# Reordering the work around the weight fold of a linear attention with a linearised MoE

## The chip, the cores and the metric

One core of a Trainium2 chip. Times are device microseconds (us) of one execution. Engines: PE is TensorE (PEld its weight loads), DVE is VectorE, ACT is ScalarE, POOL is GpSimd, SP is SyncE. The clock is the share of TensorE's full clock that the profile shows as granted. An execution counts as slow when it is over 1.5% above the fastest of the same kernel. A ratio is the mean time of one kernel's fast runs over that of the other's in the same rounds, with a 95% interval, so it is not quite the ratio of the medians.

## The reference, cut to what matters

```python
# attention: 8 batches x 8 heads x 576 positions x 64
q_p, k_p = phi(q, cos, sin), phi(k, cos, sin)      # relu(x)*cos and relu(x)*sin, side by side
kv  = einsum('bhsf,bhsd->bhfd', k_p, v);  z = sum(k_p, axis=2)
x   = einsum('bhsf,bhfd->bhsd', q_p, kv) / (q_p . z + 1e-06)
# then a feed-forward layer over 4608 tokens of 512, d_ff 2048
out = softplus(x @ w_in) @ w_out
```

The kernel replaces softplus by its line through zero: `out = x @ W_c + bias` with `W_c = 0.5 * w_in @ w_out` (the fold, 64 matmuls) and a bias of ln 2 times the column sums of `w_out`. It squares x and the weights, and branches on their norms at the end to an exact path if the line isn't good enough.

## The kernel before: the parts in question

Batch 0 is worked while the weights arrive; then W_c is copied out of PSUM; then batch 1 starts; then 32 more tiles of 128 tokens follow. Each tile has a turn of the queries (PE, copied by ACT), an attend (PE), a reciprocal and a division (DVE), a turn of x (PE, ACT) and an emit (PE with W_c; DVE adds the bias). In these traces an engine's queue is worked in the order of the program: ACT's first copy of W_c starts at 42.01 us, behind six squares, though the fold ended at 40.93.

```python
def square_w(ft):                     # norms of the weights
    if ft % 2 or ft >= 10: nc.scalar.activation(..., ACT.Square, accum_out=...)
    else:                  nc.vector.scalar_tensor_tensor(...)

def pool_relu(b):                     # GpSimd rectifies keys and queries of batch b
    nc.gpsimd.tensor_copy(gate, vcs_bufs[(b - 1) % 2][:, 3, T - 1, 1, VW - 2 :])
    ...

for j in range(BLOCKS + 1):           # the fold, 8 blocks of weights
    if j < BLOCKS: turn_w_in(j)
    ...
    if 0 < j < 5: attend(j - 1, qt_ps)
    ...
    if j > 0:
        fold(j - 1, wc_ps)
        for ft in range(FB * (j - 1), FB * j): square_w(ft)
    if j in (3, 5): sum_w_out((j - 3) // 2)
    ...
for hq in range(2):                   # the passage into batch 1
    for c in range(2): scale_values(1, hq, c)     # DVE, "value products" vcs
relu_k(1, nc.vector)
for g in range(KO): ...               # W_c out of PSUM, ACT and DVE in turn
bias()
relu_q(1, 0, nc.gpsimd); relu_q(1, 1, nc.vector)
for hq in range(2): key_values(1, hq)             # PE
finish(*emit(0, xt_bank())); turn_queries(4, split=True)
finish(*emit(1));            turn_queries(5, big_ps)
pool_relu(2)
...
def pass_stores(i, rden):             # stores wait while loads last
    keep = HOLD - 1 - 3 * max(0, i - 27)
    if len(held) > keep: nc.sync.dma_start(passed[...], rden...)   # gate copy
    while len(held) > max(0, keep): store(*held.pop(0))
```

## Time and profile before

| | before |
|---|---|
| median of the first three runs | 138.13 us (137.68 to 140.26) |
| last fold matmul ends | 40.93 us |
| first key-value product of batch 1 | 43.45 us |
| reciprocal of tile 4, 8, 13, 35 | 47.96, 57.86, 71.89, 123.81 us |
| end of the span | 136.1 us |

Here is the passage in the timeline of the kernel before (start, length, engine, line, operation, output and inputs, count, and in brackets the idle time before it and what ended it):

```profile
38.59 2.76 DVE L286 TENSOR_TENSOR vcs<-v_sb,cs_wide 128x1152 bf16<-128x1152 bf16 x4 [0.65 <-DMA v_sb<-in_v_dram]
41.42 0.76 DVE L262 TENSOR_SCALAR k_sb<-k_sb 128x2304 bf16<-128x2304 bf16 x1
42.62 1.29 DVE L496 TENSOR_SCALAR W_c<-wc_ps 128x512 bf16<-128x512 f32 x2 [0.44 <-ACT W_c L498]
42.86 1.14 POOL L269 TENSOR_SCALAR q_r<-q_sb 128x1152 bf16<-128x1152 bf16 x1 [0.19 <-DMA q_sb<-in_q_dram]
43.45 1.25 PE L300 MATMUL kv_ps<-vcs,k_sb 64*64 64x132 bf16 x72
```

### The profile page before, as it was taken

How to read it: one execution, taken by the hardware profiler on the slowest of the kernel's cores; microseconds unless marked ns; L12 is line 12 of the kernel's file. 1: busy time of each engine (PE TensorE's matmuls, PEld its weight loads, DVE VectorE, ACT ScalarE, POOL GpSimd, SP SyncE). 2: the span in 40 equal slices, each digit the busy share in tenths (PEclk: the TensorE clock that was granted, in tenths of full speed). 3: DMA queues.
4: the chain of work that ended last, by engine and by line, in shares of the span. 5: the costliest groups of instructions: out<-in, count | busy, mean ns of one | idle time of the engine just before them, and what ended most of it. 6: DMA issues, size and time to landing. Idle time of an engine off the chain costs nothing.

```text
span 136.1 us, 4522 instructions
## 1 busy us (share of the span) xinstructions
PE 114.9 (84%) x1890; PEld 74.7 (55%) x1890; DVE 102.6 (75%) x219; ACT 94.5 (69%) x161; POOL 66.5 (49%) x83
## 2 busy tenths in 40 slices
PE   5926959999699998998969998999999999989400
PEld 2303636666345665764747775766767677655100
DVE  1499536797777689999978988898977996687600
ACT  3401493696698475989876996998997997987100
POOL 6994544645525029989889666159124800000000
PEclk9999999999999999999999999999999999999985
DMA  1999999999999999999999999999996365776480
GB/s 8 179 184 200 201 202 199 200 202 202 207 207 207 208 207 210 207 209 207 208 209 207 228 262 256 253 251 256 241 277 208 117 205 200 288 245 234 180 289 15
DMA packets 24779, 28.15 MB, mean 207 GB/s; under 512 B 1712, under 2 KB 20144, under 8 KB 24752
## 3 DMA queue, kind: packets, MB, share of 16 engines
q0 software_dynamic: 19136, 18.35, 82.3%
q1 hardware_dynamic: 5616, 9.44, 20.0%
q8 instruction: 17, 0.28, 0.8%
q14 instruction: 10, 0.08, 0.2%
HBM read 36.70 MB, written 9.44 MB: 339 GB/s over the span
## 4 chain that ended last, share of the span: by engine, by line
PE 49%; DVE 22%; ACT 15%; issue 6%; POOL 2%; ACTq 0%; POOLq 0%; DVEq 0%
PE o_ps L408 11%; PE q_ps L327 9%; DVE vcs L286 8%; ACT qT L339 8%; PE wc_ps L239 8%; PE kv_ps L300 6%; PE num_ps L357 5%; PE xT_ps L377 3%; DVE o_sb L426 3%; DVE x L368 3%; ACT xT_all L381 3%; ACT x L386 3%; DVE diag L161 2%; PE wT_ps L209 2%; PE o_big L408 1%
## 5 line engine op out<-in xcount | busy, mean ns | idle before, releaser
L339 ACT CAST qT<-q_ps 128x1024 bf16<-128x1024 f32 x34 | 34.3, 1014 | 8.2 <-PE q_ps L327 8.1
L408 PE MATMUL o_ps<-W_c,xT_all 128*128 128x512 bf16 x132 | 33.9, 379 | 0.8 <-DVE o_sb L426 0.7
L286 DVE TENSOR_TENSOR vcs<-v_sb,cs_wide 128x1152 bf16<-128x1152 bf16 x32 | 28.0, 891 | 0.6 <-DMA v_sb<-in_v_dram 0.6
L426 DVE TENSOR_TENSOR o_sb<-o_ps,b_bc 128x512 f32<-128x512 f32 x33 | 22.6, 686 | 7.4 <-PE o_ps L408 7.3
L368 DVE TENSOR_TENSOR x<-num_ps,rden 128x512 bf16<-128x512 f32 x36 | 24.9, 691 | 2.1
L262 POOL TENSOR_SCALAR k_sb<-k_sb 128x1152 bf16<-128x1152 bf16 x12 | 14.9, 1253 | 17.4 <-DMA k_sb<-in_k_dram 17.4
L327 PE MATMUL q_ps<-diag,q_r 128*128 128x256 bf16 x144 | 21.9, 274 | 1.6 <-issue 0.5
L381 ACT CAST xT_all<-xT_ps 128x512 bf16<-128x512 f32 x36 | 21.4, 596 | 1.2 <-PE xT_ps L377 1.2
L269 POOL TENSOR_SCALAR q_r<-q_sb 128x1152 bf16<-128x1152 bf16 x13 | 16.8, 1305 | 6.3 <-PE q_ps L327 3.4
L386 ACT ACTIVATE x<-x,zero_b 128x1024 bf16<-128x1024 bf16 x17 | 19.7, 1161 | 0.0
L408 PEld LDWEIGHTS <-xT_all 128*128 128x128 bf16 x144 | 12.7, 98 | 10.1 <-issue 1.1
L357 PE MATMUL num_ps<-kvblk,qT 64*128 64x65 bf16 (+1 forms) x640 | 15.7, 193 | 1.1 <-issue 1.1
L327 PEld LDWEIGHTS <-q_r 128*128 128x128 bf16 x144 | 11.7, 97 | 6.0 <-issue 2.0
L239 PE MATMUL wc_ps<-w_out_sb,w_inT 128*128 128x512 bf16 x64 | 15.0, 379 | 0.0
L300 PE MATMUL kv_ps<-vcs,k_sb 64*64 64x132 bf16 x576 | 11.4, 219 | 4.1 <-DVE vcs L286 4.1
L305 ACT CAST kvblk<-kv_ps 128x260 bf16<-128x260 f32 x16 | 6.0, 375 | 10.1 <-PE kv_ps L300 9.7
L377 PE MATMUL xT_ps<-perm,x 128*128 128x128 bf16 x128 | 12.4, 219 | 0.6 <-ACT xT_all L381 0.6
L300 PEld LDWEIGHTS <-k_sb 64*64 64x64 bf16 x576 | 9.1, 106 | 6.0 <-issue 4.3
L357 PEld LDWEIGHTS <-qT 64*128 64x128 bf16 (+1 forms) x640 | 11.3, 97 | 2.0 <-issue 1.1
L377 PEld LDWEIGHTS <-x 128*128 128x128 bf16 x144 | 10.6, 98 | 2.0 <-issue 0.6
L347 PEld LDWEIGHTS <-warm 128*128 128x128 bf16 x72 | 6.7, 98 | 8.8 <-issue 1.6
L436 PE MATMUL spin_ps<-warm 128*128 128x512 bf16 x28 | 8.6, 468 | 1.5 <-DVE warm L104 1.5
(76 smaller groups left out, 131.3 us busy)
## 6 DMA issues: line engine op xcount, KB each, us to landing
out_dram<-o_sb SPq DMA_DIRECT2D x32, 256.0 KB
v_sb<-in_v_dram POOLq DMA_DIRECT2D x7, 576.0 KB, 12.2
k_sb<-in_k_dram POOLq DMA_DIRECT2D x7, 576.0 KB, 14.8
q_sb<-in_q_dram POOLq DMA_DIRECT2D x6, 576.0 KB, 18.2
xT_all<-in_moe_w_in_dram POOLq DMA_DIRECT2D x8, 256.0 KB, 10.7
w_out_sb<-in_moe_w_out_dram POOLq DMA_DIRECT2D x8, 256.0 KB, 10.7
q_sb<-in_q_dram POOLq DMA_DIRECT2D x4, 288.0 KB, 10.3
out_dram<-o_sb SPq DMA_DIRECT2D x8, 128.0 KB
```

The costliest lines, as they stand in the source:

```text
L239: nc.tensor.matmul(ps[g // 2][:, g % 2, :], w_inT_rows(ft)[:, g * 128 : (g + 1) * 128], w_out_rows(ft)[:, 0], start=(ft == 0), stop=(ft == ...
L286: nc.vector.tensor_mul(view(vcs, [T * 2 * VW, 2], [2 * VW, T], [1, D], offset=2 * hq * T * 2 * VW + c * VW), kqv[b, "v"][:, 2 * hq : 2 * h ...
L300: nc.tensor.matmul(kv[64 * i : 64 * i + 64, h2, :, :VW], k_r[rows, 2 * hq + i, t, :], vcs[rows, 2 * hq + i, t, :, :], start=(t == 0), stop ...
L327: nc.tensor.matmul(ps[:, j // 2, 256 * (j % 2) : 256 * (j % 2) + 256], q_rs[b][:, hq, t, :, :], diag[:, t, :, :], start=True, stop=True, s ...
L339: nc.scalar.copy(view(qT, [512, 2], [64, 2], [128, 4], [1, 64]), view(ps, [1, 1024]))
L357: nc.tensor.matmul(num[p0 : p0 + m, i, C * g : C * g + C], qTs[n][rows, hq, 2 * c + h2, p0 : p0 + m], blk_bufs[b % 3][rows, hq, h2, c, :], ...
L368: nc.vector.tensor_mul(xs[n // 2][:, n % 2], view(num, [C, 4], [512, 2], [1, D]), view(rden, [1, 4], [4, 2], [0, D]),)
L377: nc.tensor.matmul(ps[:, g, :], x[:, g, :, :], perm if len(tiles[n]) == 1 else ident, start=True, stop=True, skip_group_check=True,)
L381: nc.scalar.copy(xT_all[:, n], ps)
L386: nc.scalar.activation(x, x, ACT.Square, bias=zero_b, accum_out=x_norm[:, n : n + 1])
L408: nc.tensor.matmul(ps, xT_all[:, n, g, :], W_c[:, g, :], start=(g == 0), stop=(g == 3))
L426: nc.vector.tensor_add(o_sb, ps, b_bc)
```

## The change

Its intent: start the fold sooner, get W_c out sooner by moving ACT's last squares behind it, use W_c at once for four emits, and drop the gate copies of the stores. Cut to the core, in five parts that the text names **head**, **squares**, **W_c first**, **four emits** and **stores** (a load in two parts, the last half store's move to ACT's queue and the numbering of the norm's steps are cut):

```diff
 # head
+            if t < 4:  (DVE)   else:  nc.scalar.mul(diag[:, t, c, :], ident, cs_col[...])
-        spin(5)
+        spin(5 - 2 * hq)
-    turn_queries(1, big_ps)
+    turn_queries(1, big_ps, split=True)
+        if j > 0:
+            fold(j - 1, wc_ps)
         if 0 < j < 5:
             attend(j - 1, qt_ps)
 # squares: 12, 13 behind the W_c copies, 14, 15 behind the turn of tile 5, x squares 0 and 1 later
-            if j % 2 == 1:
-                square_x((j - 3) // 2)
-            for ft in range(FB * (j - 1), FB * j):  square_w(ft)      # all j
+        if 0 < j < 6:  (the same)
+        if j == 7:     (weight squares 10, 11)
 # W_c first
-    for hq in range(2): ... scale_values(1, hq, c)
-    relu_k(1, nc.vector)
     for g in range(KO): ...  W_c
+    for ft in range(6 * FB, 7 * FB):
+        square_w(ft)
     bias()
+    square_x(0)
+    for hq in range(2): ... scale_values(1, hq, c)
+    relu_k(1, nc.vector)
     relu_q(1, 0, nc.gpsimd)
-    relu_q(1, 1, nc.vector)
 # four emits
+    early = [emit(0, xt_bank()), emit(1)]
     for hq in range(2):
         key_values(1, hq)
+    (finish both, relu_q(1, 1, nc.vector), emit 2, turn 4, emit 3, turn 5, finish both)
+    for ft in range(7 * FB, FO):
+        square_w(ft)
 # stores: one gate at tile 27, on the last query load; all held stores go then
+        if i == LAST_HELD:
+            nc.sync.dma_start(passed[...], kqv[B - 1, "q"][:1, 3, T - 1, :16])
+        while len(held) > (0 if i == LAST_HELD else HOLD - 1):
```

More of the change, by code (lines that the diff above doesn't have):

```diff
@@ L124 @@
     w_tmp = loads.tile([128, 2, D_MODEL], F32, tag="q", name="w_tmp", bufs=4)
-    load(1, "v")
+    for part in range(2):
+        load(1, "v", part)
     load(1, "k")
@@ L160, in mark_diag @@
         for c in range(2):
-            nc.vector.tensor_scalar_mul(diag[:, t, c, :], ident, cs_col[:, c, t : t + 1])
+            if t < 4:
+                nc.vector.tensor_scalar_mul(diag[:, t, c, :], ident, cs_col[:, c, t : t + 1])
+            else:
+                nc.scalar.mul(diag[:, t, c, :], ident, cs_col[:, c, t : t + 1])
     perm = singles.tile([128, 128], BF16)
@@ L401, in store @@
             else:
-                nc.sync.dma_start(rows[:, T - 1, :], o_sb[p0 : p0 + m])
+                (nc.scalar if p0 and n == last else nc.sync).dma_start(
+                    rows[:, T - 1, :], o_sb[p0 : p0 + m]
+                )
     def emit(n, ps=None):
@@ L413 @@
     HOLD = 11
+    LAST_HELD = last - 8
     held = []
@@ L417, in pass_stores @@
     def pass_stores(i, rden):
-        keep = HOLD - 1 - 3 * max(0, i - 27)
-        if len(held) > keep:
+        if len(held) < HOLD or i > LAST_HELD:
+            return
+        if i == LAST_HELD:
+            nc.sync.dma_start(passed[:, i % 4, :].bitcast(BF16), kqv[B - 1, "q"][:1, 3, T - 1, :16])
+        else:
             nc.sync.dma_start(passed[:, i % 4, :], rden[:1].rearrange("p i g -> p (i g)"))
-        while len(held) > max(0, keep):
+        while len(held) > (0 if i == LAST_HELD else HOLD - 1):
             store(*held.pop(0))
@@ L427, in finish @@
         held.append((n, o_sb))
-        if n > last - 3:
-            while held:
-                store(*held.pop(0))
+        while n >= LAST_HELD - 2 and held:
+            store(*held.pop(0))
     def spin(count, rhs=None):
@@ L444 @@
     mark_eps()
-    for t in range(4):
+    for t in range(T):
         mark_diag(t)
@@ L449 @@
             relu_k(0, nc.vector, slice(2, 4))
-            for t in range(4, 8):
-                mark_diag(t)
         for c in range(2):
             scale_values(0, hq, c)
-    for hq in range(2):
         key_values(0, hq)
-        spin(5)
+        spin(5 - 2 * hq)
     for hq in range(2):
@@ L459 @@
     mark_perm()
-    mark_diag(8)
     turn_queries(0, split=True)
-    turn_queries(1, big_ps)
-    wc_ps = [None]
+    turn_queries(1, big_ps, split=True)
+    xt_bank = lambda: xt_ps.tile([128, D_MODEL], F32, tag="xt", name="o_xt")
+    big_bank = lambda: big_ps.tile([128, 2, D_MODEL], F32, tag="big", name="o_big")[:, 0]
     for j in range(BLOCKS + 1):
@@ L470 @@
             nc.vector.tensor_copy(ident_f, ident)
-        if 0 < j < 5:
-            attend(j - 1, qt_ps)
         if j == 1:
@@ L476 @@
             ]
+        if j > 0:
+            fold(j - 1, wc_ps)
+        if 0 < j < 5:
+            attend(j - 1, qt_ps)
         if 1 < j < 6:
             turn_x(j - 2)
-            if j % 2 == 1:
-                square_x((j - 3) // 2)
-        if j > 0:
-            fold(j - 1, wc_ps)
+        if 0 < j < 6:
             for ft in range(FB * (j - 1), FB * j):
+                square_w(ft)
+        if j == 7:
+            for ft in range(FB * 5, FB * 6):
                 square_w(ft)
@@ L489 @@
             fetch(3)
-    for hq in range(2):
-        for c in range(2):
-            scale_values(1, hq, c)
-    relu_k(1, nc.vector)
     for g in range(KO):
@@ L498 @@
             nc.scalar.mul(W_c[:, g, :], wc_ps[g // 2][:, g % 2, :], 0.5)
+    for ft in range(6 * FB, 7 * FB):
+        square_w(ft)
     bias()
+    square_x(0)
+    for hq in range(2):
+        for c in range(2):
+            scale_values(1, hq, c)
+    relu_k(1, nc.vector)
     relu_q(1, 0, nc.gpsimd)
-    relu_q(1, 1, nc.vector)
+    early = [emit(0, xt_bank()), emit(1)]
     for hq in range(2):
         key_values(1, hq)
-    xt_bank = lambda: xt_ps.tile([128, D_MODEL], F32, tag="xt", name="o_xt")
-    finish(*emit(0, xt_bank()))
+    for done in early:
+        finish(*done)
+    relu_q(1, 1, nc.vector)
+    early = [emit(2, xt_bank())]
     turn_queries(4, split=True)
-    finish(*emit(1))
+    early.append(emit(3))
     turn_queries(5, big_ps)
+    for done in early:
+        finish(*done)
+    for ft in range(7 * FB, FO):
+        square_w(ft)
     pool_relu(2)
@@ L542 @@
                 turn_x(i - 1)
-            if i < last:
+            if 5 < i < last:
                 finish(*emit(i - 2))
+            if i == 4:
+                square_x(1)
             if i > 4 and i % 2 == 0:
                 square_x(i // 2 - 1)
-            if b == 1 and j < 2:
-                for _ in range(1 + j):
+            if b == 1 and 1 < j < 4:
+                for _ in range(j - 1):
                     next(w_steps)
         n = mine[-1] + 1
-    big_bank = lambda: big_ps.tile([128, 2, D_MODEL], F32, tag="big", name="o_big")[:, 0]
     emitted = [emit(last - 2)]
```

## The prediction

> **What bounds the kernel now.** I read the chain that ended last, then busy time by stretches of 5 us, then the timeline at the end of the weight fold, then the queue of the stores and the last branch. The kernel has three stages: batch 0 with the weight fold (0 to 43 us), a passage into batch 1 (43 to 50), and 32 tiles of steady work (to 127), followed by the end.
>
> ```profile
> PE 49%; DVE 22%; ACT 15%; issue 6%; POOL 2%; ACTq 0%; POOLq 0%; DVEq 0%
> ```
>
> No engine owns the chain. The stretches (columns: stretch, its length, busy us and instructions of PE, PEld, DVE, ACT, POOL, then clock, DMA share, GB/s) show why:
>
> ```profile
> 35.00:40.00 5.00, 3.93 (x25) 1.99 (x24) 3.39 (x11) 3.79 (x10) 1.88 (x3) 1.00 1.21 207
> 45.00:50.00 5.00, 5.00 (x65) 3.41 (x63) 3.54 (x8) 2.66 (x4) 0.00 (x0) 1.00 1.21 208
> 55.00:60.00 5.00, 5.00 (x143) 3.59 (x131) 4.93 (x9) 4.24 (x8) 4.42 (x7) 1.00 1.21 209
> 95.00:100.00 5.00, 4.88 (x87) 3.51 (x89) 4.86 (x10) 4.75 (x9) 0.65 (x1) 1.00 1.18 248
> 105.00:110.00 5.00, 4.83 (x108) 3.55 (x106) 4.86 (x9) 4.75 (x8) 2.76 (x2) 1.00 0.30 114
> ```
>
> In the steady part PE, DVE and ACT are all over 80% busy; slack lies only in the first 50 us. The DMA is saturated (share over 1) to 105 us: the loads keep about 203 GB/s from 3 us on, and the last load releases this:
>
> ```profile
> 105.62 2.76 POOL L269 TENSOR_SCALAR q_r<-q_sb 128x1152 bf16<-128x1152 bf16 x2 [2.06 <-DMA q_sb<-in_q_dram]
> ```
>
> Batch 7's queries are rectified at 108.38, and the first turn of them starts at 110.19 in the timeline. So the computing can come forward by about 1.8 us at most before it waits for the loads.
>
> At the fold, ScalarE is late: six weight squares run before the first copy of the folded weight, which starts at 42.01 although the fold ended at 40.93.
>
> ```profile
> 20.14 0.19 PE L347 MATMUL num_ps<-eps_b,warm 128*128 128x4 bf16 x2 [1.23 <-ACT qT L339]
> ...
> 36.87 0.61 PE L209 MATMUL wT_ps<-ident,xT_all 128*128 128x128 bf16 x8 [1.07 <-ACT w_inT L215]
> ...
> 41.29 0.72 ACT L224 ACTIVATE w_square<-w_inT,zero_b 128x512 bf16<-128x512 bf16 x1
> ...
> 42.01 1.06 ACT L498 ACTIVATE W_c<-wc_ps 128x512 bf16<-128x512 f32 x2
> ```
>
> At the end SP works through a backlog of gate copies and stores, while PE has a branch that takes 4.6 us:
>
> ```profile
> 126.74 0.69 SPq L420 DMA_DIRECT2D passed<-rden  x1
> 127.84 1.85 SPq L400 DMA_DIRECT2D out_dram<-o_sb  x3
> 129.79 1.21 SPq L402 DMA_DIRECT2D out_dram<-o_sb  x2
> ...
> L566 SPq TENSOR_LOAD <-fits x1: 732/732/732, 131.1 to 131.1; - x1
> ...
> L567 PEldq COMPARE_BRANCH  x1: 4586/4586/4586, 129.6 to 129.6; - x1
> ...
> L567 SPq EVENT_SEMAPHORE  x8: 17/17/17, 132.3 to 134.4; - x8
> ...
> L567 PEldq EVENT_SEMAPHORE  x1: 51/51/51, 134.3 to 134.3; - x1
> ```
>
> Two chains meet: SP's last wait (a store) passes at 134.4 and PE comes out of its branch at 134.3. Both must be done; 1.7 us later the span ends. I take this as the most important reading: shortening SP's chain alone wins almost nothing.
>
> [...] PE's 4.59 us, and 16 KB instruction packets at 131.6 to 132.8. [...] Here, under load, the last half store was issued at 130.40 and its wait passed near 134.3: 3.9 us. [...] The trace has 1.57 us for 8 diagonals on DVE (0.20 each); none on ACT yet. [...] the value multiplies take 0.69 alone, up to 1.62 beside GpSimd at 58.70.
>
> **The change part by part.**
>
> Head. Ten diagonals leave DVE: 8 x 0.17 + 2 x 0.20 = 1.8 us. They go to ACT, which idles until 11.00[...]. DVE had waited for nothing there, but query part two lands near 13.9, so its rectifying ends at about 14.6 against 14.68. With two spins fewer the first turn of queries starts near 14.7 against 15.37: -0.7. PE's wait of 1.23 us at 20.14 is filled with the first fold. From there the weight blocks land every 2.66 us and PE needs wT 0.45 + fold 1.73 + attend 0.36 + xT 0.33 = 2.87 us a block, so I get the copy of block 5 at 30.1 (was 31.7). Behind it the unchanged DVE run of a square and three sums, 4.1 us, still holds block 6. I get the last fold's end at 39.3 against 40.93: **-1.6**.
>
> Passage. ACT now has two squares ahead of W_c: W_c starts at 38.55, and DVE's last part ends at 40.45 (was 43.91). But DVE does the value multiplies (4 x 0.69) and the key rectifying (0.76) after W_c, not before, so these end at 43.95 (was 42.18). Then two emit additions (1.38) and the query part (0.75): 46.05. The turn of tile 4 comes at 46.1 (was 45.50), and attend of tile 4 at 48.05 (was 47.36): **+0.7**, but emits 2 and 3 are done, 2 x 0.86 = 1.7 us of PE and 2 x 0.69 = 1.4 us of DVE ahead. On work done PE stands 1.0 us ahead and DVE level.
>
> ACT pays. Four weight squares (0.85 each) and two x squares (1.25) come later. Two of the former and one of the latter stand behind the turn of tile 5: 1.7 + 1.25 = 2.95 us between copies for which PE waits, because there is one bank for the turned queries. Placing the copies (0.92 each in a row): tile 6 at 51.65, tile 7 at 53.8, tile 8 at 55.3. So emit 4 ends at 55.5 against 54.3, and its addition starts about 1.0 us later than 54.49. From there to tile 11 DVE sets the pace as before, then PE. **+1.0** on the end of the computing by this placing. I trust the placing to about 1 us, and its errors are one-sided: some value multiplies leave GpSimd's windows (about 0.3), and PE's lead on the emits lets some waits overlap (about 0.3). I take **+0.4**.
>
> Gates. SP loses 8 gate copies of 0.67 us after tile 27, and all held stores go after the last load. The idle DMA at 105 to 110 us is filled. 22 stores of 0.26 MB at the 290 GB/s that the trace shows in the fast slices take 20 us, from 106 to 126, so SP is free when the last tile is. SP's chain shortens by 131.05 - 128.75 = 2.3 us (its load of the flag against the other engines'). PE's branch remains. Its fetch might gain the wait of 2.0 us from branch to packet in part, and 0.2 us of its packet (1.18 against 0.95 elsewhere), as stores drain earlier. I take **-0.8** in all, of which 0.3 is safe.
>
> Sum: +0.4 - 0.8 = -0.4; 138.13 - 0.4 = **137.7 us**.
>
> **The rivals.**
>
> 1. The squares find holes and PE's lead counts in full: the computing is 1.5 us earlier. For it: ACT is only 2.66 of 5 us busy at 45 to 50. Against: it is in order, and the squares stand where PE waits. With the tail -0.8: 135.8 us. More is cut off by the loads (1.8 us).
> 2. The passage becomes the bound: ScalarE's squares hold the single bank, DVE idles, and the placing holds in full or grows [...]. +1.0 to +1.8, tail -0.3: 138.8 to 139.6 us.
> 3. The tail is all SP: if PE's branch is short once stores are gone, 2.3 us of gain: 136.2 us. For it: the fetch packets wait behind stores. Against: the same seconds of stores also run in the new kernel.
>
> **Range and chances.** The rivals span 135.8 to 139.6. Faster by over 2% means under 135.4, which needs rivals 1 and 3 together and the loads' limit just kept: 0.13. Slower by over 2%, over 140.9, needs rival 2 beyond its top: 0.06. Within 2%: 0.81. Eight in ten: 135.7 to 139.5.
>
> **What would show it.** The fold's last matmul near 39.3; W_c on ACT near 38.6; attend of tile 4 near 48; then ACT busy nearly without a gap from 48 to 57 and PE waiting for its query copies 2 to 3 us; SP's flag load with the other engines' at the end, and PE's branch still above 4 us and last. It would be wrong if tile 4 came before 47, if PE did not wait for ACT at 49 to 54, if PE's branch fell under 3 us, or if a wait for batch 7's queries showed up near 108.

## More of the kernel before

The reciprocal of a tile is a good milepost: each tile has one, on DVE, right behind its attend. How late a milepost is tells in which stage time was lost.

DVE does batch 1's value products while PE still folds, and is done before GpSimd rectifies queries at 42.86. The key-value products begin without a wait.

## The result, and the profile after

The changed kernel took **143.09 us** in the median (141.95 to 143.69, four runs); the kernel before took 138.45 beside it. Ratio 1.0345, interval 1.0249 to 1.044: **slower**. The profiled execution took 143.19 us, its span is 140.9.

| milepost, us | before | after | later by |
|---|---|---|---|
| last fold matmul ends | 40.93 | 40.77 | -0.2 |
| first key-value product of batch 1 | 43.45 | 46.47 | 3.0 |
| reciprocal of tile 4 | 47.96 | 51.58 | 3.6 |
| reciprocal of tile 8 | 57.86 | 62.95 | 5.1 |
| reciprocal of tile 35, the last | 123.81 | 130.15 | 6.3 |
| span's end | 136.1 | 140.9 | 4.8 |

So there are three facts: 3.6 us are lost up to tile 4, nearly all of it in the passage, 2.7 more between tile 4 and the last, and 1.5 us are won back at the end. The fold gained nothing. First the fold, then the passage, in the timeline of the changed kernel:

```profile
18.82 0.62 PE L213 MATMUL wT_ps<-ident,xT_all 128*128 128x128 bf16 x8 [1.79 <-DMA xT_all<-in_moe_w_in_dram]
...
28.64 1.22 DVE L251 TENSOR_TENSOR w_sum<-w_out_sb 128x1024 f32<-128x1024 bf16 x1
...
29.77 0.42 DVE L219 COPY w_inT<-wT_ps 128x512 bf16<-128x512 bf16 x1
...
30.86 0.61 PE L213 MATMUL wT_ps<-ident,xT_all 128*128 128x128 bf16 x8 [0.49 <-ACT w_inT L219]
...
36.71 0.61 PE L213 MATMUL wT_ps<-ident,xT_all 128*128 128x128 bf16 x8 [1.12 <-ACT w_inT L219]
...
40.58 0.69 DVE L500 TENSOR_SCALAR W_c<-wc_ps 128x512 bf16<-128x512 f32 x1 [2.79 <-ACT W_c L502]
...
42.05 3.70 DVE L290 TENSOR_TENSOR vcs<-v_sb,cs_wide 128x1152 bf16<-128x1152 bf16 x4
42.99 1.47 POOL L273 TENSOR_SCALAR q_r<-q_sb 128x1152 bf16<-128x1152 bf16 x1 [0.25 <-DMA q_sb<-in_q_dram]
...
46.47 1.25 PE L304 MATMUL kv_ps<-vcs,k_sb 64*64 64x132 bf16 x72 [1.39 <-DVE k_sb L266]
...
53.98 0.66 PE L331 MATMUL q_ps<-diag,q_r 128*128 128x256 bf16 x4 [1.90 <-ACT qT L343]
```

Line 1: the second weight block is asked for sooner than it lands, and PE waits 1.79 us for it. Lines 2 to 4: a sum of 1.22 us stands ahead of the copy of a weight block in DVE's queue, and PE waits 0.49 us for that copy's partner on ACT. Line 5: behind the second run of sums PE waits again, 1.12 us, as it did in the kernel before (1.07 us at 36.87, shown in the prediction). Lines 6 to 9: DVE idles 2.79 us for W_c, and only then makes the value products; these now meet GpSimd's rectifying, take 3.70 us for 2.76, and the key-value products wait for the keys behind them. Last line: PE waits 1.90 us for a query copy that stands behind two weight squares in ACT's queue.

The stretches of the changed kernel (columns as in the prediction: PE, PEld, DVE, ACT, POOL, clock, DMA share, GB/s):

```profile
45.00:50.00 5.00, 3.62 (x87) 2.43 (x87) 3.50 (x7) 1.46 (x5) 0.12 (x1) 1.00 1.21 208
50.00:55.00 5.00, 2.95 (x54) 2.50 (x52) 4.63 (x8) 4.51 (x9) 4.32 (x4) 0.94 1.22 210
55.00:60.00 5.00, 4.64 (x90) 3.43 (x89) 2.95 (x7) 4.39 (x8) 4.42 (x7) 0.72 1.21 206
```

PE was busy 5.00 us of the same 45 to 50 before; now 3.62, then 2.95. The clock sinks to 0.72. The group of the value products, first of the kernel before and then of the changed one (count | busy, mean ns | idle before):

```profile
L286 DVE TENSOR_TENSOR vcs<-v_sb,cs_wide 128x1152 bf16<-128x1152 bf16 x32 | 28.0, 891 | 0.6 <-DMA v_sb<-in_v_dram 0.6
```

```profile
L290 DVE TENSOR_TENSOR vcs<-v_sb,cs_wide 128x1152 bf16<-128x1152 bf16 x32 | 32.0, 1017 | 0.2 <-DMA v_sb<-in_v_dram 0.2
```

The same 32 products cost 4.0 us more, and not in the passage alone. The chain of waits and the end:

```profile
PE 38%; DVE 27%; ACT 12%; DMA 8%; issue 7%; POOL 5%; POOLq 0%; DVEq 0%; ACTq 0%
```

```profile
L584 SPq TENSOR_LOAD <-fits x1: 920/920/920, 135.1 to 135.1; - x1
...
L585 PEldq COMPARE_BRANCH  x1: 3653/3653/3653, 136.1 to 136.1; - x1
...
L585 PEldq EVENT_SEMAPHORE  x1: 51/51/51, 139.8 to 139.8; - x1
```

DVE's share of the chain rose from 22 to 27%. At the end SP loads the flag with the other engines (they load at 135.1 too) and PE's branch is last, as predicted; but it took 3.65 us where the prediction wanted it above 4.

### The profile page after: what moved, and what is told of

It is laid out like the page before. It is cut to its first block, busy times and chain, and to the rows that moved or that the text cites.

```text
span 140.9 us, 4511 instructions
## 1 busy us (share of the span) xinstructions
PE 117.2 (83%) x1888; PEld 75.6 (54%) x1888; DVE 105.4 (75%) x210; ACT 97.3 (69%) x171; POOL 67.0 (48%) x84
## 4 chain that ended last, share of the span: by engine, by line
PE 38%; DVE 27%; ACT 12%; DMA 8%; issue 7%; POOL 5%; POOLq 0%; DVEq 0%; ACTq 0%
PE o_ps L414 11%; DVE vcs L290 10%; DMA xT_all<-in_moe_w_in_dram 8%; PE wc_ps L243 6%; ACT qT L343 6%; PE q_ps L331 6%; DVE o_sb L436 5%; PE kv_ps L304 5%; DVE x L372 4%; PE num_ps L361 3%; PE xT_ps L381 3%; ACT x L390 2%; PE wT_ps L213 2%; DVE w_square L233 1%; ACT xT_all L385 1%
## 5 line engine op out<-in xcount | busy, mean ns | idle before, releaser
L343 ACT CAST qT<-q_ps 128x1024 bf16<-128x1024 f32 x33 | 33.4, 1014 | 6.1 <-PE q_ps L331 5.6
L414 PE MATMUL o_ps<-W_c,xT_all 128*128 128x512 bf16 x128 | 33.1, 381 | 2.0 <-DVE o_sb L436 1.9
L290 DVE TENSOR_TENSOR vcs<-v_sb,cs_wide 128x1152 bf16<-128x1152 bf16 x32 | 32.0, 1017 | 0.2 <-DMA v_sb<-in_v_dram 0.2
L436 DVE TENSOR_TENSOR o_sb<-o_ps,b_bc 128x512 f32<-128x512 f32 x32 | 21.9, 685 | 8.3 <-PE o_ps L414 8.2
L266 POOL TENSOR_SCALAR k_sb<-k_sb 128x1152 bf16<-128x1152 bf16 x12 | 13.6, 1146 | 12.4 <-DMA k_sb<-in_k_dram 12.3
L381 PE MATMUL xT_ps<-perm,x 128*128 128x128 bf16 x128 | 12.9, 225 | 0.9 <-ACT xT_all L385 0.9
L368 DVE RECIPROCAL rden<-num_ps 128x8 f32<-128x8 f32 x36 | 7.1, 197 | 4.5 <-PE num_ps L361 4.5
```

The source lines that it names most:

```text
L290: nc.vector.tensor_mul(view(vcs, [T * 2 * VW, 2], [2 * VW, T], [1, D], offset=2 * hq * T * 2 * VW + c * VW), kqv[b, "v"][:, 2 * hq : 2 * h ...
L343: nc.scalar.copy(view(qT, [512, 2], [64, 2], [128, 4], [1, 64]), view(ps, [1, 1024]))
L381: nc.tensor.matmul(ps[:, g, :], x[:, g, :, :], perm if len(tiles[n]) == 1 else ident, start=True, stop=True, skip_group_check=True,)
L414: nc.tensor.matmul(ps, xT_all[:, n, g, :], W_c[:, g, :], start=(g == 0), stop=(g == 3))
L436: nc.vector.tensor_add(o_sb, ps, b_bc)
```

## The experiments

Eighteen kernels ran, on four chips, each with the kernel before beside it. All gave right results. "Late by" is always a reciprocal of one profiled execution against that of the kernel before.

| run | ratio | 95% interval | tile 4 late by | tile 8 | tile 35 |
|---|---|---|---|---|---|
| the change | 1.0345 | 1.0249 to 1.044 | 3.6 | 5.1 | 6.3 |
| e1 stores alone | 0.9944 | 0.9913 to 0.9974 | 0.0 | -0.2 | -0.3 |
| e7 stores, head | 0.992 | 0.9879 to 0.996 | -0.6 | -0.1 | -0.3 |
| e2 change, W_c first undone | 1.0254 | 1.0205 to 1.0303 | 2.1 | 3.6 | 3.4 |
| e3 change, squares early | 1.0171 | 1.011 to 1.0233 | 3.6 | 1.9 | 0.9 |
| e4 change, both | 1.0084 | 1.0052 to 1.0116 | 4.3 | 4.4 | 3.1 |
| e5 = e4, bias earlier | 0.9931 | 0.99 to 0.9962 | 3.1 | 1.8 | 1.6 |
| e6 = e5, two emits | 1.0087 | 1.0051 to 1.0122 | 2.3 | 3.2 | 2.4 |
| e9 before, squares | 1.0051 | 1.0009 to 1.0092 | 0.1 | 1.6 | 1.2 |
| e10 before, W_c first | 1.0455 | 1.0345 to 1.0564 | 6.4 | 7.5 | 5.9 |
| e15 = e10, four emits | 1.0303 | 1.017 to 1.0435 | 4.6 | 4.8 | 3.5 |
| e11 = e7, four emits | 0.9981 | 0.9942 to 1.002 | 2.0 | 1.2 | -0.5 |
| e13 change, clock held | 1.0245 | 1.0141 to 1.0348 | 3.5 | 5.0 | 5.9 |
| e17 change, later gate | 1.0253 | 1.017 to 1.0335 | 4.5 | 4.5 | 4.3 |

The profiles of e5, e7 and e13 fell on slow executions. Those of e4, e12, e16 and e17 lost part of TensorE's clock between 10 and 24 us (0.50 in their worst slices of 2 us, 0.56 in e16), and their fold ended at 41.83 to 42.88 us, 1.0 to 2.0 us later than the same fold in the kernel that each was made from; their lateness contains that. (e2, e5, e6, e13 and e18 lost it too, from 10 to about 14 us, and ended the fold in time.) Tile 4 is also a rough milepost for kernels with four emits: in all of them tile 5 is about 1.1 us less late than tile 4 (the change: 2.5 us). e8, e12, e14, e16 and e18 are told below.

**Undoing parts of the change (e1 to e4).** My theory was that W_c first and the late squares cost together what the change lost; the rival was the four emits or the head.

```diff
 # e1: the kernel before, with the stores' part alone
 # e2: the change, with
+    (scale_values(1), relu_k(1))  ahead of the W_c copies again
 # e3: the change, with
-    for ft in range(6 * FB, 7 * FB): square_w(ft)
+    for ft in range(6 * FB, FO): square_w(ft)      # and square_x(0), square_x(1) behind the bias
 # e4: e2 and e3
```

> The kernel before with only the change of the stores (one gate, all held stores behind the last load, the last half store on ACT). Theory A (the stores' change is good, the loss is all in the passage): the end after the last reciprocal shrinks from 12.3 us to about 10.8 as in the changed kernel, so 1.0 to 1.5 us faster than before, about 137. Rival B (the stores' change delays the steady part, by holding back or by bursts): no gain or a loss of 1 us or more, with tile 35's reciprocal later than 123.8.

> The changed kernel with the value multiplies and the key rectifying of batch 1 put back ahead of the copies of the folded weight on DVE. Theory A (DVE's new order is half of the loss: it waits 2.8 us for W_c, then the multiplies meet GpSimd's rectifying): batch 1's key products start near 44 in place of 46.5, attend of tile 4 near 48 in place of 50.3, the time about 2 to 2.5 us under the changed kernel's 143.1. Rival C (the loss is the head: late first block, sum ahead of the copy): under 0.7 us of gain.

> The changed kernel with the last two weight squares and the second x square put in ACT's idle time before the turn of tile 4, and none between the query copies. Theory A: PE's wait of 1.9 us for the query copy at 54 goes, the granted clock stays at 1.00 at 50 to 60, and tile 7's lag on tile 4 falls from 7.7 us to about 6; 1.5 to 2.5 us under 143.1. Rival C: under 0.7 us. Rival B: no change.

> Both of the last two. Theory A: the gains add, 3.5 to 5 us under 143.1, so 138 to 139.5, and with the shorter end near or just under the kernel before. Rival C or B: still 2 us or more above the kernel before.

Measured: the stores alone win 0.6%. Undoing W_c first brings back 0.9% of the 3.45% (about 1.3 us, less than expected, and within the two intervals, which overlap), undoing the squares' place 1.7%, both 2.6%. What kept e4 from parity is in its timeline: four squares now stand ahead of the copy of the bias on ACT.

```profile
45.61 0.57 ACT L261 ACTIVATE b_bc<-b_ps 128x512 f32<-128x512 f32 x1
46.21 0.69 DVE L436 TENSOR_TENSOR o_sb<-o_xt,b_bc 128x512 f32<-128x512 f32 x1 [2.83 <-ACT b_bc L261]
```

DVE idles 2.83 us for it. That was a fault of my edit, and it led to the next run.

**Repairing the change (e5, e6).**

```diff
 # e5: e4 with the bias' copy ahead of squares 14, 15
     for ft in range(6 * FB, 7 * FB): square_w(ft)
     bias()
+    for ft in range(7 * FB, FO): square_w(ft)
 # e6: e5 with the passage's emits as in the kernel before (two, and later)
```

> The kernel of the last run (values first, squares early) with the bias copy on ACT put ahead of the last two weight squares. That run showed PE waiting 0.96 us and DVE 2.8 us for the bias copy behind four squares. Theory A: those waits go, attend of tile 4 near 48.5 in place of 51, 0.8 to 1.5 us faster than that run, about 137 (ratio to before about 0.995 to 1.00). Rival C (the head is what still costs): no change, ratio 1.008.

> The last kernel with two emits in the passage, as before, in place of four: only the squares' places, the head and the stores then differ from the kernel before. If four emits are a gain (work moved into idle time): 0.5 to 1.5 us slower than the last kernel. If they are what still costs (tile 4 comes late for them): as much faster, about 136.3, ratio 0.99.

e5 is at 0.9931, a little faster than before and level with the stores alone (e1): three moves in two in-order queues take away the whole loss of 3.45%. In this setting the four emits are a good thing: without them e6 is at 1.0087, and the two intervals don't meet.

**The head (e7, e8).**

```diff
 # e7: e1 with the head's part
 # e8: e7 with the sum of w_out's second part behind the last weight turn
-        if j in (3, 5):  sum_w_out((j - 3) // 2)
+        if j in (3, 7):  sum_w_out(j // 7)         # and the order of bias' two terms swapped
```

> The kernel before with the stores' change and the head alone: diagonals on ACT, folds ahead of the tiles, split copy, two spins fewer; nothing of the passage. Theory A: the head is worth little, since the fold's end moved by 0.2 us only (40.9 to 40.7) - the copies wait for DVE's sums: ratio 0.992 to 0.996, as the stores alone (0.9944). Rival C: the head costs 1 us: ratio near 1.00.

> The last kernel with the second half of the column sums of the output weight moved on DVE from ahead of the copy of block 6 to behind that of block 7, and the bias product's use of them last. If DVE's sums hold the fold: the fold ends near 39.5 in place of 40.7; PE gains up to 1 us there. But DVE then does 3.1 us of sums where it did batch 1's values, so the gain may be taken back: key products near 44.5 to 46. Ratio 0.985 if the fold's end counts, 0.995 to 1.005 if DVE bounds the passage.

e7: 0.992 against e1's 0.9944, intervals nearly the same, so the head's gain isn't resolved. Its fold ended at 40.09 us; in e11 and e18, with the same head, at 40.65 and 40.46. e8 was a bad build: 1.2066. The sum's buffers come from the ring that loads the queries, and so late it waited for GpSimd to be done with one:

```profile
54.43 1.23 DVE L250 TENSOR_TENSOR w_tmp<-w_out_sb 128x1024 f32<-128x1024 bf16 x1 [17.38 <-POOL q_r L272]
```

But its fold ended at 39.82 us, 1.1 before the kernel before, the earliest of all 20 kernels. That agrees with the reading that DVE's sums hold the fold.

**One part alone on the kernel before (e9, e10), and emits on the repaired head (e11, e12).**

```diff
 # e9: the kernel before + squares      # e10: the kernel before + W_c first
 # e11: e7 + four emits                 # e12: e1 + four emits
```

> The kernel before with one part of the change alone: weight squares 12 and 13 behind the last fold, 14 and 15 behind the query turn of tile 5, the first two x squares behind the bias and in the loop. Theory (the late squares cost by themselves: they stand on ScalarE ahead of the query copies that TensorE waits for): 1.0 to 2.5 us slower, ratio 1.007 to 1.018, with a matmul of queries after 50 us that waits over 1 us for a ScalarE copy, and a granted TensorE clock under 1.00 in one of the slices from 50 to 60 us. Rival (they hurt only because the changed kernel is late in the passage already): ratio 0.997 to 1.004 and no such wait. Fold's end within 0.3 us of 40.9 in both.

> The kernel before with one part alone: on VectorE the halves of W_c go ahead of the value products and the key rectifying of batch 1. Theory (VectorE idles for the end of the fold and then does 4 us of batch 1's work that it could have done before): the key-value products of batch 1 begin 1.5 to 3 us later than 43.4 us and the total is 1.0 to 2.2 us longer, ratio 1.007 to 1.016. Rival (TensorE has other work there and takes it up later): they begin later but the ratio is 0.997 to 1.004.

> The kernel of the run on stores and head, with the four emits of the passage added; squares and value products stay where the kernel before has them. Theory (the four emits are a gain of about 1.5% wherever the passage isn't late, as taking them out of a repaired kernel cost 1.6%): ratio 0.977 to 0.985. Rival (they only paid back what the late squares cost): ratio 0.989 to 0.996, as that run had without them.

> The kernel of the run on the stores alone, with the four emits of the passage added, without the head's part. If the head gives nothing, as theory has it (the fold's end is set by when its weights are turned on VectorE and ScalarE): ratio within 0.003 of the run with stores, head and four emits. If the head is worth the 0.3% by which the two earlier runs differ or more: at least 0.003 higher than that.

e9: 1.0051, between the two forecasts. PE waits 1.35 us for a query copy at 51.02 as expected, but its clock stays at 1.00, so that half of the theory fell. e10 was the surprise: W_c first **by itself** costs 4.55%, more than the whole change, where I had expected 0.7 to 1.6%. The stretches and the timeline of e10 say why:

```profile
45.00:50.00 5.00, 2.70 (x74) 2.23 (x75) 2.91 (x5) 0.75 (x2) 0.28 (x1) 0.61 1.21 208
50.00:55.00 5.00, 5.00 (x40) 2.87 (x38) 2.69 (x5) 1.64 (x3) 3.93 (x4) 0.71 1.21 207
```

```profile
42.62 1.29 DVE L492 TENSOR_SCALAR W_c<-wc_ps 128x512 bf16<-128x512 f32 x2 [4.67 <-ACT W_c L494]
...
47.30 2.19 PE L300 MATMUL kv_ps<-vcs,k_sb 64*64 64x132 bf16 x72 [3.79 <-DVE k_sb L262]
```

DVE idles 4.67 us and then has the products to do; PE has nothing in between, stands still for 3.79 us, and comes back at a lower clock: 0.61 is granted from 45 to 50 us, and the 72 products take 2.19 us for 1.25. So the 4.55% holds a lost clock too. Other holes, told at e12, do not order by length.

e11 gave 0.9981: four emits win nothing where values are on time (e7 without them: 0.992; the intervals overlap). So I read their 1.6% in e5 as the filling of a hole that the change itself had made: in e6 PE waits 1.31 us at 48.31 for a copy on ACT that stands behind the squares, and in e5 it has no wait above 0.70 us there. e12 (median 140.5 us, ratio 1.0133, 0.9997 to 1.0268) was unclear, and its profile is not usable for the passage: the clock had already gone at the start. Its first spin ended early, PE idled 3.21 us ahead of the first key-value products, and:

```profile
10.00:12.00 2.00, 1.77 (x40) 1.02 (x40) 2.00 (x11) 0.38 (x1) 1.14 (x2) 0.84 1.21 203
12.00:14.00 2.00, 1.37 (x26) 0.73 (x28) 2.00 (x5) 0.00 (x0) 0.79 (x2) 0.50 1.32 199
```

e1, the same there, idled 3.04 us at that place and kept 1.00. The length of the hole does not decide it, though: e11 kept it after 2.93 us, while e13 and e18 idled only 2.00 and 2.02 us at this place and lost the clock (0.60 and 0.59 from 10 to 12 us). In the passage, too, after a wait of 1.90 us ahead of the same turn of queries, the change lost it (0.59 and 0.55 from 54 to 58 us) and e17 kept it (1.00 from 50 to 60). By what rule the clock falls, these runs don't show.

**Is it the clock? (e13 to e16).** After e10 I believed that a lost clock explained why the parts don't add, and, lost at the start, the scatter of every kernel (136 to 144 us for the kernel before). In the change the granted clock is 1.00 up to 54 us and 0.50 from 55 to 57, behind PE's waits of 1.39 and 1.90 us; that these waits bring it down was my theory.

```diff
 # e13: the change, with matmuls of no use in PE's two holes
     early = [emit(0, xt_bank()), emit(1)]
+    spin(6)
...
+            if i == 5:
+                spin(8, pool=o_ps)
             if i + LEAD <= last:
 # e14: e5, e16: the kernel before, each with
-    spin(18)
+    spin(24)
 # e15: e10 + four emits
```

> The changed kernel with matmuls of no use put where TensorE stands idle in the passage: six behind the emits of tiles 0 and 1, eight ahead of the query turn of tile 7. Theory (about 1.6 us of the loss is the granted TensorE clock[...]): the granted clock is 1.00 from 50 to 60 us, the waits for ScalarE and VectorE are the same, and the time is 1.0 to 2.0 us under the changed kernel's 143.1, ratio to before 1.020 to 1.027. Rival (the clock dip only lengthens matmuls beside waits that would have stood anyway): ratio 1.030 or more although the clock is 1.00.

> The repaired kernel (values first, all squares early, bias ahead of the last squares, four emits, stores) with 24 instead of 18 matmuls in the warming spin at the start. Theory (executions whose spin ends over 3.2 us before the first key-value products lose the clock there and are the slow ones): the spread of the runs shrinks, none has a mean clock under 0.975, and the median is 135.6 to 136.4 us; ratio of fast runs 0.989 to 0.994. Rival (the slow executions have another cause): highest run still over 139 us, median as without it (136.9).

> The kernel before with two parts: values behind W_c as in the run that cost 4.5%, and the four emits. Theory (without the emits ahead of them TensorE idles 3.8 us and loses its clock; with two emits in that hole it doesn't): the clock stays at 1.00 from 45 to 55 us and the ratio is 1.015 to 1.028. Rival (the late key-value products set the loss, whatever fills the hole): ratio 1.035 to 1.050.

> The kernel before with 24 instead of 18 matmuls in the warming spin, nothing else. Theory (as in the run of the repaired kernel with the longer spin): no mean clock under 0.970, highest run under 140 us where before reaches 143 to 144, median 136.2 to 137.2; ratio of fast runs 0.995 to 1.001, since the fast runs of before had the clock. Rival: spread and median as before (138.5).

e15 bears it out in part for e10: with two emits in the hole, PE's idle time is 2.14 us, the clock stays at 1.00, and tile 4 is 4.6 us late instead of 6.4. Its ratio, 1.0303, lies between the two forecasts, and the emits also move work forward, so the clock's share alone is not shown. But e13 spoke against it for the change. Its stretches:

```profile
50.00:55.00 5.00, 4.78 (x77) 3.17 (x75) 4.73 (x8) 4.62 (x9) 4.21 (x4) 1.00 1.22 210
55.00:60.00 5.00, 4.17 (x84) 2.97 (x78) 3.85 (x8) 4.80 (x8) 4.40 (x7) 1.00 1.21 206
```

The clock is whole, and yet tile 8 is 5.0 us late, as in the change (5.1), and the last tile 5.9 (6.3). The clock was not free on the way: at tile 7 e13 is 3.3 us late and the change 4.2. That lead is gone at tile 8, because the value products between them end at the same time in both, as the next part shows. In the timed rounds e13's ratio, 1.0245, lies in the range that the theory had named, its median was 141.31 us, and its six runs had mean clocks of 0.973 to 0.992 where the change's four had 0.962 to 0.972; but the ratio's interval overlaps with the change's. So I can't say from times whether the clock is worth nothing or up to 1%; the profiles say that nothing of it is left at tile 8.

The scatter wasn't the spin. The 3.2 us of e14's theory lay between the hole of e1 (3.04 us, clock kept) and those of e12 and e5 (3.21 and 3.42, clock lost). e14's median is 137.0 us and its highest 141.63; e16's are 138.44 and 143.29, ratio 0.9993. The hole at the start was filled (0.46 and 0.90 us of idle time left), and slow runs came all the same. So this hole is not what makes the slow runs. Whether a clock lost elsewhere is, stays open: e16's own profile lost it at another place (0.56 and 0.59 from 20 to 24 us) and ended the fold at 42.38 us for 40.93, and no run filled that hole.

**A meeting of two engines (e17, e18).** The table shows a step between tiles 4 and 8 in some kernels and not in others. GpSimd starts to rectify batch 3's keys at 58.1 to 59.1 us in all kernels but e8 and e17, early and late ones alike; its wait ends with the load of the keys. A kernel that is on time has the last pair of batch 2's value products done by then (before: 55.92 to 57.34). The change runs into it; so does e13, whose pair starts 0.9 us sooner and ends no sooner (62.19 us for 62.23):

```profile
58.69 2.26 POOL L266 TENSOR_SCALAR k_sb<-k_sb 128x1152 bf16<-128x1152 bf16 x2 [0.58 <-DMA k_sb<-in_k_dram]
60.11 2.12 DVE L290 TENSOR_TENSOR vcs<-v_sb,cs_wide 128x1152 bf16<-128x1152 bf16 x2
```

```profile
59.21 2.98 DVE L290 TENSOR_TENSOR vcs<-v_sb,cs_wide 128x1152 bf16<-128x1152 bf16 x2
```

To take the meeting away I let GpSimd's little gate copy read what the last value product wrote:

```diff
-        nc.gpsimd.tensor_copy(gate, vcs_bufs[(b - 1) % 2][:, 3, T - 1, 1, VW - 2 :])
+        nc.gpsimd.tensor_copy(gate, vcs_bufs[(b - 1) % 2][:, 3, T - 1, 1, :2])
 # e17: in the change;  e18: in e7
```

> The changed kernel with GpSimd's little copy ahead of each batch's rectifying reading what the last value product wrote, so that the rectifying starts behind the products and not beside them. Theory (the passage is 3 us late and then falls on GpSimd's rectifying of batch 3, which starts at 58.1 to 58.8 us in every kernel since a load sets it; the pair of value products then takes 2.1 to 3.3 us for 1.42): the pair takes under 1.6 us, the reciprocal of tile 8 is at most 4.2 us later than in before (5.1 in the changed kernel), and the ratio falls by 0.005 or more, to 1.029 or less. Rival (GpSimd's later start only delays loads and keys): ratio 1.033 or more.

> The run of stores and head, the best so far (0.992), with the same later gate. If the collisions of value products and rectifying still cost something where the passage is on time: ratio 0.980 to 0.989. If its products already run free of them where it matters: 0.990 to 0.997.

e17's timeline and its group of value products:

```profile
60.17 1.42 DVE L290 TENSOR_TENSOR vcs<-v_sb,cs_wide 128x1152 bf16<-128x1152 bf16 x2
61.72 0.19 POOL L282 COPY gate<-vcs 128x2 bf16<-128x2 bf16 x1 [4.30 <-DVE vcs L290]
```

```profile
L290 DVE TENSOR_TENSOR vcs<-v_sb,cs_wide 128x1152 bf16<-128x1152 bf16 x32 | 28.4, 904 | 0.6 <-DMA v_sb<-in_v_dram 0.6
```

The pair takes 1.42 us, GpSimd waits for it, and all 32 products take 28.4 us, near the 28.0 of before (the change 32.0, e13 32.8). The lateness hardly grows any more: 4.5 us at tile 4, 4.5 at tile 8, 4.3 at the last, where the change went 3.6, 5.1, 6.3; from tile 5, 0.9 us in e17 and 3.9 in the change. The other profiles agree: from tile 7 to tile 8 the lateness steps up by 0.9 to 2.1 us in the seven kernels whose pair takes 2.12 to 3.30 us beside GpSimd (the change, e2, e4, e6, e12, e13, e15), and by at most 0.3 in the ten whose pair takes 1.41 or 1.42. (e10, whose products are not in the same place, steps by 0.8.) Most of that step is gone again by tile 10 (3.8 us late in the change, 4.2 in e17). What stays comes at a later meeting: from tile 17 to 18 the change loses 1.3 us, where a product of 0.75 us takes 2.59 at 86.58 beside the rectifying; e17 loses nothing there. (Tile 8 missed the 4.2 that I had asked for; this execution was already 1.8 us later than the change's at tile 3, as its fold ended at 42.35.) Why a product takes longer beside GpSimd, the traces don't show; that it does, they do: 1.42 us for this pair alone, 2.12 and 2.98 beside the rectifying. The timed ratio, 1.0253, is lower than the change's, but the intervals overlap: the gain is shown by the profile, not by the times. In e18, where values are on time, the gate is no help: 1.0003 (0.9969 to 1.0037) against e7's 0.992, outside both forecasts. How much worse it is, is less sure than the intervals say: the cut for a fast run lies 1.5% above the fastest of each kernel, so one run moves it (12 of e7's 22 runs count, 21 of e18's 22). Medians of all runs over those of the kernel before beside them are 0.989 for e7 and 0.992 for e18. Its reciprocal of tile 13 is 1.8 us ahead of the kernel before and that of tile 27 only 0.3: the lead is lost in between, and I didn't follow up to what.

The best kernels are e7 (0.992), e5 (0.9931) and e1 (0.9944). They can't be told apart, and each beats both kernels, the kernel before by under 1%.

## Why the prediction was wrong

- **Head, "-1.6".** Failed: -0.2. I had the copy of block 5 at 30.1 us, "was 31.7"; it came at 31.56. From block 2 to 3 the head was 0.9 us ahead (turns at 21.50 and 24.40 for 22.37 and 25.27), as the reordering intended. (The ten diagonals took 3.02 us on ACT, 0.30 each; the trace before had shown none there.) That lead was lost at DVE's first sum, which stands ahead of the next block's copy: that copy came at 29.77 where it had been at 28.91, because the attend now comes behind the fold and the division ahead of the sum came later with it (27.42 for 26.56). I had reckoned only with the second run of sums. Nor did I see the wait for the second weight block (1.79 us): in the kernel before, the same arrival was hidden behind other waits, so the trace did not show it as one.
- **Passage, "+0.7".** Failed, and this is the step that decides: tile 4's attend came at 50.38, +3.0 (it was to come at 48.05). The order of events was as predicted, but the term for the value products rested on the -1.6. DVE's last part of W_c ended 1.7 us after the 40.45 that I had put, and 4 x 0.69 us became 3.70, as the products slid onto GpSimd's rectifying of queries. I had seen in the trace before that a product takes up to 1.62 us beside GpSimd for 0.69, but used that only for later products. And I counted W_c first as neutral work moved, when it leaves DVE idle for the end of the fold: e10 shows 4.55% for that alone, lost clock included.
- **"PE stands 1.0 us ahead", the emits.** The lead was real work in a hole of the change's own making (e5 against e6; e10 against e15 by their profiles, as the intervals overlap). Where there is no hole it is worth nothing measurable (e11 against e7).
- **ACT pays, "+1.0", taken as "+0.4".** The kind was right: PE waited 1.90 us for a query copy behind the squares. The size was too small, and I had discounted it with arguments that the trace didn't carry. Undone in the change it brings 1.7% back (e3), about 2.4 us. Alone on the kernel before it costs 0.5%, about 0.7 us (e9). A late passage is not the whole reason for the difference: with the value products early the same squares still cost 1.7% (e2 against e4). The rest stays open.
- **A term that was missing.** Between tile 4 and the last, 2.7 us more were lost. The prediction had lateness carried along, not growing. It grew by 1.7 us from tile 5 to tile 7, where PE waits behind the squares (1.90 us) and its clock falls (0.72 from 55 to 60 us), by 0.9 at tile 8, most of which came back, and by 1.3 at tile 18. The last two steps are value products that fell on GpSimd's rectifying, whose start, at tile 8, a load sets; in e17, where the meeting is removed, both are gone (0.3 and 0.0). e3 shows the same growth gone when the squares no longer push the products that far: 3.6, then 0.9.
- **Gates, "-0.8".** Right. e1 gives 0.56%, 0.8 us, and SP loads the flag with the others, with PE's branch last. The branch itself became shorter: 4.29 to 4.59 us in the five kernels with the old stores, 3.34 to 4.01 in the fifteen with the new. (That the branch waits for instruction packets was my estimate from their place: in the kernel before one of 16 KB is under way from 131.62 to 132.80 us, inside the branch's 129.6 to 134.2.)
- **The rivals.** Rival 2 (the passage as the bound) is what happened, with value products slowed beside GpSimd's rectifying (3.70 us for 2.76), but its top, 139.6 us, fell short, as it rested on the same fold end. Of the checks that I named, "attend of tile 4 near 48" failed, and so did the fold's end near 39.3 and the branch above 4 us. None of the four signs of being wrong came true: as far as they spoke of tile 4, they looked for it too early, not too late.

Not settled: how much of the 3.45% is the clock's (nothing to 1% by the times), how much of it is the split load, which I never ran alone, what makes the clock fall, and what causes slow executions.

## What to carry to other kernels

Before moving work behind something that an engine has to wait for, ask what that engine will do until then: work that was free while it waited comes out on the critical path, as the value products did (the key-value products behind them began at 46.47 us for 43.45). A move can be undone by one instruction that still stands ahead in an engine's queue (a sum of 1.22 us ahead of a weight block's copy; in e4 the squares ahead of the bias, for which DVE idled 2.83 us), so follow each moved result to the first engine that needs it. And a stage that becomes late doesn't only shift: it can slide onto work that a load has fixed in time (batch 3's keys, which GpSimd began to rectify at 58.1 to 59.1 us in 18 of the 20 kernels), so try the parts alone and together; here their costs did not add.
